# One call for each quarter of the hidden layer in place of one for two, in a convolution with top-1 mixture of experts

## The chip, the cores and the metric

The kernel runs on one core of a Trainium2 chip. The metric is the device time of one execution in microseconds (us). A core has five engines with a queue of instructions each: TensorE (PE, with its weight loads shown apart as PEld), VectorE (DVE), ScalarE (ACT), GpSimd (POOL) and SyncE (SP), which here only starts DMAs. [...]

## What is computed

`x` is 8 x 3584 rows of 192 numbers, 28,672 rows in all. First a causal convolution of 7 taps: each of 8 heads (24 columns each) has its own 7 weights, normalised by a softmax. Then a layer of 8 experts, of which each row uses one:

```python
logits = x @ w_gate                      # x is here the convolution's result
e_idx = np.argmax(logits, axis=1)
gate_w = softmax(logits)[row, e_idx]
eom = 1.0 / (1.0 + np.exp(-(x @ w_output_gate)))
for e in range(E):
    h = np.maximum(x[mask] @ w1[e], 0.0)   # 192 -> 1024
    ye = h @ w2[e]                         # 1024 -> 192
    out[mask] = gate_w[mask, None] * eom[mask, e, None] * ye
```

## The kernel before

**Front end.** The rows are cut into 16 units of 1,792 rows. For a unit, `front_a` does the convolution as 8 matmuls in float32 with banded weights (L290; each shows as two matmul records), copies the results out of PSUM as `cv`, transposes them with 24 small matmuls in 6 groups (L304), copies these as `tt`, multiplies by the gate weights (L313, a tile of 32 columns) and transposes back (L322). `front_b` finds each row's expert and weight on VectorE, counts with small matmuls (L361, L383 to L386), works out each row's place in its expert's stream (the rank chain, VectorE, L389 to L409), and then sorts the rows by permutation matmuls: `prep` makes the scaled rows `xrow` (L423) and the permutation `pm` (L428) on VectorE, L444 multiplies them, the result is copied out as `xs` (L278 on ScalarE or L280 on VectorE, in turn), and GpSimd scatters it to `xcg_sorted` in HBM (L462). Both are Python generators: each `yield` is a step that the main loop can place between other work.

**Slots.** A slot is 512 consecutive rows of one expert's stream, read back transposed as two overlapping pieces: `xa` holds columns 0 to 127, `xb` columns 64 to 191. Each unit from the third on has 4 slots, the last unit 8 and then 3 of 256 rows whose expert is chosen at run time (`pick`, L534 to L565, on VectorE). A last loop takes up what is left. `first` is the product 192 -> 1024. The 1024 hidden columns are four quarters of 2 x 128. Each of these two halves needs a matmul over 128 rows (`xa` or `xb`, L613) and one over the other 64 (L620): `xb[64:128]` or `xa[0:64]`[...]. A quarter takes one PSUM buffer `pp`[...]; the pool has two. A relu moves it to SBUF as `ht`: quarter 3 on VectorE (L631), the others on ScalarE (L633). `second(q)` is the product 1024 -> 192 for 128 of the rows: 8 matmuls of 192 columns (L655), and after each odd `q` a copy `y` (L661), which GpSimd scatters to the output (L482).

**Order of the work.** It is written out by hand; PE runs what it is given in that order. In the main loop a unit has 16 positions, `pos = 4 * k + q` for slot `k` and quarter `q`. At each position stand, in this order: `first` (before: at even `q` only, for two quarters), one step of `front_a` of the unit after next (positions 0 to 7 an L290, 8 to 10 an L304 group, 11 the L313), `second(q)` of the slot before, and then one step of the next unit's sort (positions 0 to 7), a second step of `front_a` (8 to 11: L304, at 11 L322) or a step of the following `front_b` (12 to 15: experts, counts, rank chain, first two `prep`). The small PSUM tiles of the front end, `pf`, have two buffers.

```python
for q in range(4):
    pos = 4 * k + q
    if q % 2 == 0:
        s.first(q // 2)
    drain(fa, 1)
    if prev is not None:
        prev.second(q)
```

Of the kernel before, what the change touches and what calls it, by code (L numbers as in the profile page):

```python
# [11 lines left out]
FP16 = mybir.dt.float16  # L12
FP32 = mybir.dt.float32
U32 = mybir.dt.uint32
AF = mybir.ActivationFunctionType
# [6 lines left out]
def kernel(  # L22
# [10 lines left out]
    nc = tc.nc  # L33
# [4 lines left out]
    F = moe_w1.shape[2]  # L38
# [10 lines left out]
    TT = 512  # L49
# [25 lines left out]
    ph = ctx.enter_context(tc.tile_pool(name="ph", bufs=2))  # L75
    pp16 = ctx.enter_context(tc.tile_pool(name="pp16", bufs=4))
    py = ctx.enter_context(tc.tile_pool(name="py", bufs=3))
    ps_h = ctx.enter_context(tc.tile_pool(name="ps_h", bufs=2, space=bass.MemoryType.PSUM))
# [60 lines left out]
    for h in (0, H // 2):  # L139
        for k in range(KW):  # L140
            m = idpu[:, k:k + BT]
            nc.vector.copy_predicated(
                out=band[:, h:h + H // 2, :],
# [60 lines left out]
    def load_w(e):  # L204
        o = e * WE
        w = moe_w1[e]
        nc.gpsimd.dma_start(
            wres[:, o:o + F].rearrange("p (l c) -> p l c", l=2),
            bass.AP(tensor=w.tensor, offset=w.offset,
                    ap=[[F, 128], [64 * F + F // 2, 2], [1, F // 2]]))  # L210
        nc.gpsimd.dma_start(wres[0:64, o + F:o + WA], w[0:64, F // 2:F])
        nc.gpsimd.dma_start(wres[64:128, o + F:o + WA], w[128:D, 0:F // 2])
        nc.gpsimd.dma_start(
            wres[:, o + WA:o + WE].rearrange("p (c d) -> p c d", d=D),
            moe_w2[e].rearrange("(c p) d -> p c d", p=128))
# [22 lines left out]
        out=o9, in_=bass.AP(tensor=eqe.tensor, offset=eqe.offset,  # L238
                            ap=[[eqe.ap[0][0], GE], [0, NG], [1, E + 1]]),
# [4 lines left out]
    for l in range(2):  # L244
        nc.vector.tensor_scalar(
            out=lsum[:, l * GE:(l + 1) * GE].rearrange("p (i e) -> p i e", e=E),
# [4 lines left out]
        out=lsum[:, c0 + NSEG:c0 + 2 * NSEG].rearrange("p (i e) -> p i e", e=E + 1),  # L251
# [216 lines left out]
    def emit_in(n=1):  # L468
        while n and pend:
            if last[0] == "in":  # L470
                nc.gpsimd.nop()
            pend.popleft()()
            last[0] = "in"
            n -= 1
# [3 lines left out]
    def emit_out():  # L478

        while pout:  # L480
            y, oi, j = pout.popleft()
            i = nc.gpsimd.indirect_dma_start(  # L482
                out=out, out_offset=bass.IndirectOffsetOnAxis(ap=oi[:, j:j + 1], axis=0),
                in_=y[:, j, :], in_offset=None, bounds_check=N - 1, oob_is_err=False)
            nodep(i, "out", ("out",))
            last[0] = "out"
# [81 lines left out]
    def slot_load(base, u, n=TT):  # L568
        skip = [f"sc{v}" for v in range(u + 1, NU)]
        xa = pxt.tile([128, TT], FP16, tag="xa", name="xa")[:, 0:n]  # L570
        xb = pxt.tile([128, TT], FP16, tag="xb", name="xb")[:, 0:n]
        xi = pxt.tile([128, 4, 2], FP16, tag="xi", name="xi")[:, 0:n // 128]
        i = nc.sync.dma_start_transpose(xa, xcg[bass.ds(base, n), 0:128])
        nodep(i, "load", skip)
        i = nc.sync.dma_start_transpose(xb, xcg[bass.ds(base, n), 64:192])
        nodep(i, "load", skip)
        i = nc.sync.dma_start(
            xi, xcg[bass.ds(base, n), IDC:IDC + 2].rearrange("(j p) w -> p j w", p=128))
        nodep(i, "load", skip)
        return xa, xb, xi  # L580
# [3 lines left out]
    def w_dyn(sel):  # L584

        if not wds:
            t = px.tile([128, NB, D], FP32, tag="xt", name="wd")
            t = t.rearrange("p c d -> p (c d)").bitcast(FP16)
            wds.extend(t[:, i * WE:(i + 1) * WE] for i in range(2 * NB * D // WE))
        wd = wds.pop(0)  # L590
        nc.sync.dma_start(wd, wres[:, bass.ds(reg(sel[0:1, 0:1], [ET.SP], (E - 1) * WE), WE)])
        return wd


    class Slot:
# [4 lines left out]
            self.nq = self.n // 128  # L600
            self.ht = []

        def first(self, q2):

            n, w = self.n, self.w
            pps = [ps_h.tile([128, 2, 512], FP32, tag="ph", name="pp")[:, :, 0:n]
                   for _ in range(2)]

            def rows128(r):
                o = (2 * q2 + r) * 128  # L610
                for l, x in enumerate((self.xa, self.xb)):
                    o2 = l * (F // 2) + o
                    nc.tensor.matmul(pps[r][:, l, :], w[:, o2:o2 + 128], x,  # L613
                                     start=(r == 0), stop=(r == 1))

            def rows64(r):

                c = F + (2 * q2 + r) * 128
                for l, (x, p0) in enumerate(((self.xb, 64), (self.xa, 0))):
                    nc.tensor.matmul(pps[r][:, l, :], w[p0:p0 + 64, c:c + 128], x[p0:p0 + 64],  # L620
                                     start=(r == 1), stop=(r == 0))

            rows128(0)
            rows64(0)
            rows64(1)
            rows128(1)
            for r in range(2):
                q = 2 * q2 + r
                ht = ph.tile([128, 2, TT], FP16, tag=f"ht{q}", name=f"ht{q}")[:, :, 0:n]
                if q == 3:  # L630
                    nc.vector.tensor_relu(out=ht, in_=pps[r])  # L631
                else:
                    nc.scalar.activation(out=ht, in_=pps[r], func=AF.Relu)  # L633
                self.ht.append(ht)

        def second(self, q):
            if q >= self.nq:
# [27 lines left out]
    def reg(ap, engines, hi):  # L665
        return nc.values_load(ap, engines=engines, min_val=0, max_val=hi,
                              skip_runtime_bounds_check_because="computed row of the stream")


    def drain(g, n=None):  # L670
        k = 0
        while n is None or k < n:
            try:
                next(g)
            except StopIteration:
                return False
            k += 1
        return True
# [9 lines left out]
    for u in range(U0 + 1):  # L688
# [5 lines left out]
        if u == 0:  # L694
# [3 lines left out]
            for e in range(E):  # L698
                i = nc.sync.dma_start(
                    out=xcg[e * CAP:e * CAP + TT, :].rearrange("(p g) w -> p (g w)", g=GR), in_=zrow)  # L700
# [4 lines left out]
    def loads(u):  # L705
        todo = []
        for e, bap, inv in plans.pop(u):
            base = reg(bap, [ET.SP], E * CAP - TT)
            todo.append((wres[:, e * WE:(e + 1) * WE], inv, slot_load(base, u)))
        if u == NU - 1:  # L710
            for sel, bap, inv in [pick(TP // 2) for _ in range(ND)]:
                base = reg(bap[0:1, 0:1], [ET.SP], E * CAP - TT)
                todo.append((w_dyn(sel), inv, slot_load(base, u, TT // 2)))
        return todo
# [11 lines left out]
    for u in range(U0, NU):  # L726
        fs, fa, fbn = fbn, iter(()), iter(())
        if u + 2 < NU:
            fa, fbn = front_a(u + 2), front_b(u + 2)
        nxt = None  # L730
        for k, (w, inv, xabi) in enumerate(todo):
            if 0 < 4 * (u - U0) + k <= EH:
                load_w(EH - 1 + 4 * (u - U0) + k)
            s = Slot(xabi, w, inv)
            for q in range(4):
                pos = 4 * k + q
                if q % 2 == 0:
                    s.first(q // 2)
                drain(fa, 1)
                if prev is not None:  # L740
                    prev.second(q)
                    emit_out()
                if pos < 8:
                    drain(fs, 1)
                elif pos < 12:
                    drain(fa, 1)
                else:
                    drain(fbn, 1)
                emit_in(len(pend))
                if pos == 7 and u + 1 < NU:  # L750
                    nxt = loads(u + 1)
            prev = s
        todo = nxt
# [20 lines left out]
    with tc.For_i(0, rn, 1):  # L774
        sel, bou, iu1 = pick(TP)
        base = reg(bou[0:1, 0:1], [ET.SP], E * CAP - TT)
        wds.clear()
        s = Slot(slot_load(base, NU), w_dyn(sel), iu1)
        for q2 in range(2):
            s.first(q2)  # L780
        for q in range(4):
            s.second(q)
            emit_out()
# [30 lines left out]
```

## Time and profile before

| | |
|---|---|
| median of 3 runs | 646.91 us (646.39 to 647.25) |
| the profiled execution | 647.25 us |
| its span on the core | 645.5 us |
| matmuls of `first`, 128 rows (L613, 512 columns) | 480, in 240 + 240 |
| matmuls of `first`, 64 rows (L620, 512 columns) | 480 |
| relus (L633 ScalarE, L631 VectorE) | 189 of 1001 ns, 63 of 1185 ns |
| matmuls of `second` (L655) | 1,968 |
| TensorE clock granted | 0.981 of full speed |

The page gives busy time by engine, the span in slices, the DMA queues, the chain of work that ended last, and groups of instructions by line. The end of a matmul's record is modelled and matmuls overlap, so how long TensorE is held is read between the starts of two matmuls that follow each other. "Idle before" is time in which an engine waited, and the name after the arrow is what released it.

### The profile page before, as it was taken

The page shows a single profiled execution, that of the slowest core. Times are in us where ns is not written, and L with a number is a line of the kernel's source. Part 1 is how long each engine was busy: PE and PEld are TensorE (multiplying, and loading weights), DVE is VectorE, ACT ScalarE, POOL GpSimd, SP SyncE. Part 2 cuts the span into 40 slices and gives each one's busy share as a digit, 9 for nine tenths or more (in the row PEclk, how much of TensorE's full clock was granted, in tenths as well). Part 3 has the DMA queues.
Part 4 walks back from the last instruction along what each step waited for, and adds up shares of the span by engine and source line. Part 5 has one row for each costly group of instructions (what it writes and reads, how often), then busy time and mean ns, then how long its engine had stood idle before and what let it go on. Part 6 is the DMA issues. An engine that isn't in the chain of part 4 may idle for free.

```text
span 645.5 us, 13578 instructions
## 1 busy us (share of the span) xinstructions
PE 586.5 (91%) x4544; PEld 360.3 (56%) x4544; DVE 406.3 (63%) x1362; ACT 355.4 (55%) x586; POOL 401.5 (62%) x419
## 2 busy tenths in 40 slices
PE   3998739999999999999999999999999999979993
PEld 1554415656665566656566566655566565546662
DVE  7567536584957658494775849577594956943332
ACT  1676525554665555556555555555555565656661
POOL 1362726876775756667476655756566674777773
PEclk9999859999999999999999999999999999999997
DMA  6979439994654647264553637355372525246631
GB/s 160 191 186 258 132 76 201 143 211 137 138 169 117 176 106 171 85 153 131 117 155 101 185 87 165 105 114 165 92 188 88 107 82 113 73 108 136 188 115 37
DMA packets 162569, 88.14 MB, mean 137 GB/s; under 512 B 116765, under 2 KB 153792, under 8 KB 162496
## 3 DMA queue, kind: packets, MB, share of 16 engines
q1 hardware_dynamic: 131872, 43.92, 30.3%
q0 software_dynamic: 29728, 43.30, 25.8%
q8 instruction: 36, 0.59, 0.4%
q14 instruction: 37, 0.30, 0.2%
q10 hardware_dynamic: 896, 0.03, 0.1%
HBM read 35.92 MB, written 43.06 MB: 122 GB/s over the span
## 4 chain that ended last, share of the span: by engine, by line
PE 66%; DVE 19%; ACT 6%; DMA 4%; issue 3%; SPq 0%; POOL 0%; DVEq 0%; ACTq 0%; POOLq 0%
PE pyt L655 18%; PE pp L613 13%; PE pf L290 11%; PE pp L620 8%; PE pf L444 5%; DVE ht L631 5%; PE pf L313 5%; PE pf L304 5%; ACT ht L633 4%; DVE xrow L423 2%; DVE pm L428 2%; DVE cv L280 2%; PE pf L322 2%; DMA out_dram<-y,oi 1%; DMA xt<-in_x_dram 1%
## 5 line engine op out<-in xcount | busy, mean ns | idle before, releaser
L482 POOL DMA_INDIRECT out_dram<-y,oi x246 | 245.6, 998 | 127.6 <-ACT y L661 63.4
L633 ACT ACTIVATE ht<-pp 128x1024 f16<-128x1024 f32 (+1 forms) x189 | 183.1, 1001 | 69.8 <-PE pp L620 67.0
L655 PEld LDWEIGHTS <-ht 128*128 128x128 f16 x1968 | 166.6, 98 | 58.2 <-issue 29.5
L655 PE MATMUL pyt<-wres,ht 128*128 128x192 f16 x1920 | 192.7, 246 | 1.5 <-DVE ht L631 1.5
L462 POOL DMA_INDIRECT xcg_sorted<-xs,du x128 | 131.5, 1027 | 92.2 <-DVE tk L502 22.1
L290 PE MATMUL pf<-xt,band 118*112 118x384 f32 x256 | 109.4, 523 | 19.1 <-DMA xt<-in_x_dram 10.8
L631 DVE TENSOR_SCALAR ht<-pp 128x1024 f16<-128x1024 f32 (+1 forms) x63 | 74.7, 1185 | 71.8 <-PE pp L613 71.8
L661 ACT COPY y<-pyt 128x384 f32<-128x384 f32 x123 | 59.0, 479 | 85.6 <-PE pyt L655 84.1
L613 PE MATMUL pp<-xa,wres 128*128 128x512 f16 x240 | 92.9, 387 | 9.1 <-DMA xa<-xcg_sorted 9.1
L613 PE MATMUL pp<-xb,wres 128*128 128x512 f16 x240 | 91.3, 380 | 1.2 <-DMA xb<-xcg_sorted 1.2
L620 PE MATMUL pp<-xb,wres 64*128 64x512 f16 x240 | 73.0, 383 | 1.6 <-ACT ht L633 1.2
L620 PE MATMUL pp<-xa,wres 64*128 64x512 f16 x240 | 73.0, 383 | 0.0
L444 PE MATMUL pf<-xrow,pm 112*128 112x194 f16 x512 | 65.1, 249 | 5.8 <-DVE pm L428 4.1
L613 PEld LDWEIGHTS <-wres 128*128 128x128 f16 x480 | 34.8, 97 | 60.7 <-issue 59.7
L290 PEld LDWEIGHTS pf<-xt,band 118*112 118x112 f32 x256 | 42.5, 185 | 41.6 <-DVE cv L280 11.5
L278 ACT COPY cv<-pf 112x384 f32<-112x384 f32 x80 | 38.1, 478 | 46.5 <-PE pf L290 38.6
L428 DVE TENSOR_SCALAR pm<-pos,pos 112x256 f16<-112x256 f16 x256 | 62.1, 307 | 0.0
L423 DVE TENSOR_TENSOR xrow<-cv,gs 112x384 f16<-112x384 f32 x121 | 61.9, 551 | 0.0
L444 PEld LDWEIGHTS <-pm 112*128 112x128 f16 x512 | 44.7, 98 | 15.3 <-DVE pm L428 7.7
L304 PE MATMUL pf<-identf,cv 112*128 112x112 f32 x384 | 50.7, 260 | 2.3 <-ACT tt L278 2.1
L278 ACT CAST xs<-pf 128x388 f16<-128x388 f32 x76 | 37.1, 492 | 27.5 <-PE pf L444 27.5
L304 PEld LDWEIGHTS pf<-identf,cv 112*128 112x128 f32 x384 | 40.9, 141 | 10.0 <-ACT tt L278 3.4
(139 smaller groups left out, 447.2 us busy)
## 6 DMA issues: line engine op xcount, KB each, us to landing
xt<-in_x_dram SPq DMA_DIRECT2D x8, 1344.0 KB
xt<-in_x_dram SPq DMA_DIRECT2D x8, 1260.0 KB
out_dram<-y,oi POOLq DMA_INDIRECT x246
wres<-in_moe_w_dram POOLq DMA_DIRECT2D x8, 384.0 KB
wd<-wres SPq DMA_DIRECT2D x3, 768.0 KB
wres<-in_moe_w_dram POOLq DMA_DIRECT2D x8, 256.0 KB
xcg_sorted<-xs,du POOLq DMA_INDIRECT x128
xcg_sorted<-zrow SPq DMA_DIRECT2D x8, 256.0 KB
```

Of the source, the lines that this page charges most:

```text
L278: nc.scalar.copy(out=o, in_=i)
L290: nc.tensor.matmul(pc[0:BT, 0:NB * GH], band[0:KI, h, :], xt[0:KI, :, h * GH:(h + 1) * GH], start=True, stop=True)
L304: nc.tensor.matmul(pt[:, j * BT:(j + 1) * BT], cvf[0:BT, m * 2 * D + i * 128:m * 2 * D + (i + 1) * 128], identf[0:BT, 0:BT], is_transpose= ...
L428: nc.vector.tensor_scalar(out=pms[i][P, l, :], in0=pos16[P], scalar1=pos[P, l * NG + i:l * NG + i + 1], scalar2=None, op0=ALU.is_equal)
L444: nc.tensor.matmul(ps[:, r * XW:(r + 1) * XW], pm[P, l, r * 128:(r + 1) * 128], xr[P, l * NG + i, :], start=(r == 0 and l == 0), stop=(r = ...
L462: i = nc.gpsimd.indirect_dma_start(out=xcg2, out_offset=bass.IndirectOffsetOnAxis(ap=du[:, i:i + 1], axis=0), in_=xs.rearrange("p r w -> p ...
L482: i = nc.gpsimd.indirect_dma_start(out=out, out_offset=bass.IndirectOffsetOnAxis(ap=oi[:, j:j + 1], axis=0), in_=y[:, j, :], in_offset=Non ...
L613: nc.tensor.matmul(pps[r][:, l, :], w[:, o2:o2 + 128], x, start=(r == 0), stop=(r == 1))
L620: nc.tensor.matmul(pps[r][:, l, :], w[p0:p0 + 64, c:c + 128], x[p0:p0 + 64], start=(r == 1), stop=(r == 0))
L631: nc.vector.tensor_relu(out=ht, in_=pps[r])
L633: nc.scalar.activation(out=ht, in_=pps[r], func=AF.Relu)
L655: nc.tensor.matmul(self.pp[:, o:o + D], self.ht[fc // 2][:, fc % 2, q * 128:(q + 1) * 128], self.w[:, w:w + D], start=(fc == 0 and q % 2 = ...
```

## The change

`first` takes one quarter `q` and is called at every position. Its matmuls run in the order 128 rows, 128 rows, 64 rows, 64 rows, and its relu follows at once. Before, a call took two quarters, in the order 128, 128, then four of 64 rows, then 128, 128, and the two relus followed. The loop at the end changes in the same way. Nothing else changes.

```diff
-        def first(self, q2):
-
+        def first(self, q):
             n, w = self.n, self.w
-            pps = [ps_h.tile([128, 2, 512], FP32, tag="ph", name="pp")[:, :, 0:n]
-                   for _ in range(2)]
...
-            rows128(0)
-            rows64(0)
-            rows64(1)
-            rows128(1)
-            for r in range(2):
-                q = 2 * q2 + r
...
+            o, o2, c = q * 128, F // 2 + q * 128, F + q * 128
+            pp = ps_h.tile([128, 2, 512], FP32, tag="ph", name="pp")[:, :, 0:n]
+            nc.tensor.matmul(pp[:, 0, :], w[:, o:o + 128], self.xa, start=True, stop=False)
+            nc.tensor.matmul(pp[:, 1, :], w[:, o2:o2 + 128], self.xb, start=True, stop=False)
+
+            nc.tensor.matmul(pp[:, 0, :], w[64:128, c:c + 128], self.xb[64:128],
+                             start=False, stop=True)
+            nc.tensor.matmul(pp[:, 1, :], w[0:64, c:c + 128], self.xa[0:64],
+                             start=False, stop=True)
+            ht = ph.tile([128, 2, TT], FP16, tag=f"ht{q}", name=f"ht{q}")[:, :, 0:n]
+            if q == 3:
+                nc.vector.tensor_relu(out=ht, in_=pp)
+            else:
+                nc.scalar.activation(out=ht, in_=pp, func=AF.Relu)
+            self.ht.append(ht)
@@
             for q in range(4):
                 pos = 4 * k + q
-                if q % 2 == 0:
-                    s.first(q // 2)
+                s.first(q)
                 drain(fa, 1)
@@
-        for q2 in range(2):
-            s.first(q2)
+        for q in range(4):
+            s.first(q)
         for q in range(4):
             s.second(q)
             emit_out()
```

More of the change, by code (lines that the diff above doesn't have):

```diff
@@ L601, in __init__ @@
             self.ht = []
-        def first(self, q2):
+        def first(self, q):
             n, w = self.n, self.w
-            pps = [ps_h.tile([128, 2, 512], FP32, tag="ph", name="pp")[:, :, 0:n]
-                   for _ in range(2)]
[L609 to L621, printed above, removed]
-            rows128(0)
-            rows64(0)
-            rows64(1)
-            rows128(1)
-            for r in range(2):
-                q = 2 * q2 + r
[L629 to L634, printed above, removed]
+            o, o2, c = q * 128, F // 2 + q * 128, F + q * 128
[12 more added lines that the diff above has]
+            self.ht.append(ht)
         def second(self, q):
```

## The prediction

> **What bounds the kernel now.** I read the page first: span, busy shares, chain.
>
> ```profile
> span 645.5 us, 13578 instructions
> PE 586.5 (91%) x4544; PEld 360.3 (56%) x4544; DVE 406.3 (63%) x1362; ACT 355.4 (55%) x586; POOL 401.5 (62%) x419
> PE 66%; DVE 19%; ACT 6%; DMA 4%; issue 3%; SPq 0%; POOL 0%; DVEq 0%; ACTq 0%; POOLq 0%
> ```
>
> TensorE carries two thirds of the chain. The busy table by stretch says where it is full:
>
> ```profile
> 300.00:400.00 100.00, 97.40 (x782) 60.23 (x780) 67.57 (x220) 56.33 (x90) 61.01 (x62) 1.00 0.49 125
> ```
>
> The columns are length, then PE, PE's loads, DVE, ACT and POOL. From 92 us to 621 us PE sets the pace, so each 0.1 us added to its order is paid. [...] The timeline of PE over one call of `first(q2)`:
>
> ```profile
> 300.79 0.38 PE L613 MATMUL pp<-xa,wres 128*128 128x512 f16 x1
> 301.01 0.38 PE L613 MATMUL pp<-xb,wres 128*128 128x512 f16 x1
> 301.32 0.39 PE L620 MATMUL pp<-xb,wres 64*128 64x512 f16 x1
> 301.32 0.39 PE L620 MATMUL pp<-xa,wres 64*128 64x512 f16 x1
> 301.54 0.38 PE L620 MATMUL pp<-xb,wres 64*128 64x512 f16 x1
> 301.55 0.38 PE L620 MATMUL pp<-xa,wres 64*128 64x512 f16 x1
> 301.85 0.39 PE L613 MATMUL pp<-xa,wres 128*128 128x512 f16 x1
> 302.08 0.38 PE L613 MATMUL pp<-xb,wres 128*128 128x512 f16 x1
> 302.30 0.55 PE L304 MATMUL pf<-identf,cv 112*128 112x112 f32 x4
> ```
>
> A 128-row matmul takes 0.22 us. Two 64-row ones start together and share one 0.22. Where the row count changes the step is 0.31: 0.09 more, on entering 64 rows (301.01 to 301.32) and on leaving (301.54 to 301.85). Over the trace the median steps are 310 and 308 ns (120 of each). Every other change of tile shape pays the same: L386 (64 rows) to L655 158 ns for 66 of work, L313 (32 columns) to L655 472 for about 376, L304 to L313 188 against 95.
>
> PE also waits, inside pairs of positions. Position 2k+1 has no first product, so its L290 follows L444 at once and finds its PSUM tile not yet copied out:
>
> ```profile
> 287.82 0.50 PE L444 MATMUL pf<-xrow,pm 112*128 112x194 f16 x4
> 289.06 0.90 PE L290 MATMUL pf<-xt,band 118*112 118x384 f32 x2 [0.73 <-DVE cv L280]
> ```
>
> [...] the L613 load starts at 300.70, ahead of its matmul; the loads of the two changes start with theirs, at 301.31 and 301.85; the 64-row matmuls start together at 301.32. [...] Here an f32 load of L290 takes 177 ns, an f16 one 98. [...]
>
> **The change, part by part.** The matmuls, relus and bytes are the same; no DMA is issued or moved. [...] Sums are against the profiled execution, 647.25 us (span 645.5 and 1.75 around it); the median of the runs is 646.91, 0.34 lower.
>
> (a) *Tile changes.* Before, a pair takes 1.505 us from its first start to the next work (median steps; 1.51 above). After, a quarter takes 0.22 + 0.31 + 0.00 + 0.31 = 0.84 to the start of the next work, two take 1.68: +0.175. There are 60 slots of 512 rows, 120 pairs: +21.0. The three half slots pay 0.16 for each of 6 pairs: +1.0. Where `first(3)` now stands directly before L313, the change to 32 columns was paid anyhow: -0.09 in each of 12 units, -1.1. Sum +20.9.
>
> (b) *Weights loaded in the open.* What now follows the 64-row matmuls is no longer always an f16 load. Where L290 started after a wait, with its load not ahead of it, its second matmul came 410 ns later instead of 326 (30 times): +0.085. L304 in that case 151 for 100 (6 times): +0.05. L655 after a known change of shape 93 for 82: +0.01. Each unit with a front has 8 exits to L290 and 3 to L304: 96 x 0.085 = 8.2, 36 x 0.05 = 1.8, 48 exits to L655 0.5. One L290 in each unit is hidden by wait (d), -1.0; the 30 and 6 of today go with their waits, -2.9. Sum +6.6. No run shows an f32 load after a 64-row tile. Bounds: 0 added [...] (then only the -2.9 stays), 9.5 [...]; I take the upper[...].
>
> (c) *Waits that go.* With a `first(q)` of 0.84 us between L444 and the next L290, and between L304 and L304 or L313, the copy has that time. By start-to-start steps over 92 to 545 us, L444 to L290 exceeds its 82 ns by 13.4 in all (longest 0.90), L304 to L304 its 95 by 3.4, L304 to L313 its 188 by 2.9. None is longer than 0.90, so I take 19.5 of the 19.7 as gone. ScalarE, with one relu (0.97) ahead of a copy in place of two, helps. Bounds: 15 if copies also come later, 19.7.
>
> (d) *Waits that come.* The relu of quarter 3 is VectorE's and moves one position later. At position 15 it now stands behind the rank chain of position 14 (L389 to L409), ahead of the first `xrow` and `pm` of the next unit's sort:
>
> ```profile
> 278.22 1.16 DVE L631 TENSOR_SCALAR ht<-pp 128x1024 f16<-128x1024 f32 x1
> ...
> 278.76 0.23 PE L386 MATMUL pf<-lsum,np 64*128 64x152 f16 x1
> ...
> 279.30 0.28 DVE L389 TENSOR_TENSOR dm<-pf,msk 112x128 f32<-112x128 f32 x1
> ...
> 281.89 0.99 DVE L428 TENSOR_SCALAR pm<-pos,pos 112x256 f16<-112x256 f16 x4
> 282.40 0.50 PE L444 MATMUL pf<-xrow,pm 112*128 112x194 f16 x4
> ```
>
> From L386's start: today the first `pm` is ready after 3.6 us and L444 starts after 3.64, no slack. After: rank chain 0.26 to 1.9, relu to 3.07, `xrow` (1.02) and two `pm` (0.49) to 4.42. PE reaches L444 after 0.16 + 0.84 + 0.66 + 0.84 + 0.74 + 0.66 = 3.9. Wait 0.5 to 0.55, 12 times: +6.6. Behind L444 stands all of PE's order. The same relu stands ahead of the `cv` copy in position 3; by the same walk it makes L290 of position 4 late by 0 to 0.5 in the six units whose `cv` copies are VectorE's: +1.5. Bounds of (d): 0 (another free PSUM tile and slack found) to 12.
>
> (e) *After 545 us*. Three `pick`s (14 VectorE instructions each, 561.4 to 569.6) hold the relu; PE's 3.3 us of waits there start with `loads` at position 7 and stay. Two waits for xa and xb at 575 (0.66 and 0.65) become shorter, -1.0; the last slots find quarter 3's relu closer to its use, about +0.3 each for three. I take 0. The loop at the end runs no round in this trace.
>
> Evacuation keeps up: a full slot after takes at least 6.0 us, ScalarE needs 3 x 0.97 + 2 x 0.48 = 3.9. A `pp` buffer is wanted again two calls later (3.0 us at the least), its relu ends 2.0 to 2.2 after the call's start.
>
> Sum: 20.9 + 6.6 - 19.5 + 8.1 + 0 = +16.1: 663.4 in the profiled run's terms, 663.0 against the median.
>
> **Rivals.** *R1[...].* (b) turns to -2.9, and PE, earlier, waits a little more in (d): 20.9 - 2.9 - 19.5 + 9 = +7.5, about 654.5 (651 to 657). [...] Against: an f32 load is 80 ns longer, and the open ones above show it.
> *R2, faster: even spacing wins.* The fused stage loses about 25 us to waits within units (2.1 in each of 12). If all of them go, no load is exposed and VectorE's shorter queue removes (d): 22 - 1.1 - 25.6 - 1.3 = -6, 641. It decides where the waits removed exceed the 20.9 of tile changes. Against it: the waits that a spacing of 0.84 us can touch sum to 19.7, below 20.9 before any exposed load.
> *R3, VectorE becomes the bound.* It is busy without a gap from 280.5 to 289 in the units that copy `cv` on it. If its late relu also stops `second(0)` of the next slot at fc 6, some 0.7 for half of the slots, +10 to +15 more: 675.
> *R4, no change*: (b) and (d) both near 0 in a sum of +1 or less.
>
> **How the numbers follow.** Chances: forecast 0.60 (its own range 657.5 to 669), R1 0.21, R2 0.06, R3 0.09, R4 0.04. The range 651 to 670 holds the forecast and R1, about 8 in 10. A measurement here can tell 0.2%, 1.3 us, from no change: faster 0.06, same 0.04, slower 0.90.
>
> **What would show it.** (a) After the change 252 entries and 252 exits with steps near 0.31, no 64-row pair followed by another. (b) The first L290 step after an exit near 0.41, not 0.33. (c) No [.. <-DVE cv] wait at odd positions. (d) A PE wait `<-DVE pm` at L444 at the start of each unit, near 0.5. A unit today takes 37.8 us (288.08 to 363.61 for two); I expect 38.9. Wrong if exits cost nothing where the shape changes back, or if a unit stays at 37.8.

## The result, and the profile after

The changed kernel takes 664.03 us (661.77 to 666.40, four runs) against 646.65 us for the kernel before: 1.027 times as long, with a 95% interval of 1.023 to 1.031. The forecast was 663.0. The profiled execution took 664.28 us, its span is 662.5, 17.0 more than before. Where a kernel's runs fall into a faster and a slower group, ratios in this document compare the faster ones.

The page after, the same three lines as before (span, busy shares, shares of the chain):

```profile
span 662.5 us, 13521 instructions
PE 614.9 (93%) x4544; PEld 363.5 (55%) x4544; DVE 409.4 (62%) x1362; ACT 356.0 (54%) x586; POOL 397.6 (60%) x419
PE 77%; DVE 13%; DMA 4%; issue 2%; ACT 1%; POOL 1%; SPq 0%; ACTq 0%; DVEq 0%; POOLq 0%
```

VectorE, ScalarE and GpSimd are as busy as they were, within 4 us. TensorE is busy 28 us longer with the same 4,544 matmuls, and its share of the chain rises from 66% to 77%. The timeline of PE over one quarter shows why (in the changed kernel L607 to L612 are the matmuls of `first`, L616 and L618 its relus on VectorE and ScalarE, and L640 is `second`, L655 before):

```profile
242.72 0.39 PE L607 MATMUL pp<-xa,wres 128*128 128x512 f16 x1
242.95 0.38 PE L608 MATMUL pp<-xb,wres 128*128 128x512 f16 x1
243.26 0.39 PE L610 MATMUL pp<-xb,wres 64*128 64x512 f16 x1
243.26 0.39 PE L612 MATMUL pp<-xa,wres 64*128 64x512 f16 x1
243.58 0.83 PE L640 MATMUL pyt<-wres,ht 128*128 128x192 f16 x8
```

242.72 to 243.58 is 0.86 us for one quarter (0.85 by the median steps), where a pair took 1.51. Both of its last two steps, 0.31 and 0.32, hold a change of tile shape, and there are 252 quarters.

Cut at the last L386 of a unit, the 17.0 us lie as follows. To the fifth unit's mark (127.76 us before, 126.13 after) 1.6 us are won. The eleven units to the last mark take 427.1 in place of 416.1, +11.0: two units together 77.65 in place of 75.53. From there to the last matmul it is 98.1 for 90.4, +7.7. What follows the last matmul is 11.3 in both. The cut itself shifts 0.85 us: quarter 3 of the slot stands ahead of this L386 before and behind it in the changed kernel. So the start wins 0.8 rather than 1.6, and the end loses 6.8 rather than 7.7.

### The profile page after: what moved, and what is told of

The parts are those of the page before. It is cut to its first block, busy times and chain, and to the rows that moved or that the text cites. A ratio compares the mean times of both kernels' runs of the same rounds, so it can differ in the third digit from the quotient of the medians.

```text
span 662.5 us, 13521 instructions
## 1 busy us (share of the span) xinstructions
PE 614.9 (93%) x4544; PEld 363.5 (55%) x4544; DVE 409.4 (62%) x1362; ACT 356.0 (54%) x586; POOL 397.6 (60%) x419
## 4 chain that ended last, share of the span: by engine, by line
PE 77%; DVE 13%; DMA 4%; issue 2%; ACT 1%; POOL 1%; SPq 0%; ACTq 0%; DVEq 0%; POOLq 0%
PE pyt L640 21%; PE pf L290 13%; PE pp L610 10%; PE pp L607 7%; PE pp L608 7%; PE pf L304 6%; PE pf L444 6%; PE pf L313 4%; DVE xrow L423 3%; DMA out_dram<-y,oi 2%; DVE ht L616 2%; DVE pm L428 2%; PE pf L322 1%; DVE xs L280 1%; DMA wg<-n_moe_w_output_gate_dram 0%
## 5 line engine op out<-in xcount | busy, mean ns | idle before, releaser
L482 POOL DMA_INDIRECT out_dram<-y,oi x246 | 244.8, 995 | 149.8 <-ACT y L646 87.6
L618 ACT ACTIVATE ht<-pp 128x1024 f16<-128x1024 f32 (+1 forms) x189 | 189.5, 1003 | 104.9 <-PE pp L612 103.8
L640 PE MATMUL pyt<-wres,ht 128*128 128x192 f16 x1920 | 200.2, 247 | 4.0 <-DVE ht L616 4.0
L640 PEld LDWEIGHTS <-ht 128*128 128x128 f16 x1968 | 160.7, 98 | 71.2 <-issue 51.5
L462 POOL DMA_INDIRECT xcg_sorted<-xs,du x128 | 128.4, 1003 | 90.4 <-DVE tk L502 22.7
L290 PE MATMUL pf<-xt,band 118*112 118x384 f32 x256 | 115.0, 545 | 10.6 <-DMA wg<-n_moe_w_output_gate_dram 10.6
L616 DVE TENSOR_SCALAR ht<-pp 128x1024 f16<-128x1024 f32 (+1 forms) x63 | 75.5, 1198 | 67.0 <-PE pp L612 66.0
L607 PE MATMUL pp<-xa,wres 128*128 128x512 f16 x240 | 92.3, 384 | 8.8 <-DMA xa<-xcg_sorted 8.8
L612 PE MATMUL pp<-xa,wres 64*128 64x512 f16 x240 | 93.6, 390 | 0.0
L610 PE MATMUL pp<-xb,wres 64*128 64x512 f16 x240 | 93.6, 390 | 0.0
L610 PEld LDWEIGHTS <-wres 64*128 64x128 f16 x240 | 22.2, 92 | 103.8 <-issue 103.8
L444 PE MATMUL pf<-xrow,pm 112*128 112x194 f16 x512 | 66.3, 249 | 7.6 <-DVE pm L428 7.2
L290 PEld LDWEIGHTS pf<-xt,band 118*112 118x112 f32 x256 | 38.2, 183 | 40.5 <-issue 21.4
L280 DVE COPY tt<-pf 128x448 f32<-128x448 f32 x36 | 22.5, 625 | 53.4 <-PE pf L304 53.4
L444 PEld LDWEIGHTS <-pm 112*128 112x128 f16 x512 | 44.3, 98 | 20.1 <-DVE pm L428 13.0
L304 PE MATMUL pf<-identf,cv 112*128 112x112 f32 x384 | 53.3, 265 | 0.2 <-ACT cv L278 0.2
```

The lines of the kernel that those rows point to most:

```text
L290: nc.tensor.matmul(pc[0:BT, 0:NB * GH], band[0:KI, h, :], xt[0:KI, :, h * GH:(h + 1) * GH], start=True, stop=True)
L304: nc.tensor.matmul(pt[:, j * BT:(j + 1) * BT], cvf[0:BT, m * 2 * D + i * 128:m * 2 * D + (i + 1) * 128], identf[0:BT, 0:BT], is_transpose= ...
L444: nc.tensor.matmul(ps[:, r * XW:(r + 1) * XW], pm[P, l, r * 128:(r + 1) * 128], xr[P, l * NG + i, :], start=(r == 0 and l == 0), stop=(r = ...
L462: i = nc.gpsimd.indirect_dma_start(out=xcg2, out_offset=bass.IndirectOffsetOnAxis(ap=du[:, i:i + 1], axis=0), in_=xs.rearrange("p r w -> p ...
L482: i = nc.gpsimd.indirect_dma_start(out=out, out_offset=bass.IndirectOffsetOnAxis(ap=oi[:, j:j + 1], axis=0), in_=y[:, j, :], in_offset=Non ...
L607: nc.tensor.matmul(pp[:, 0, :], w[:, o:o + 128], self.xa, start=True, stop=False)
```

## The experiments

Two theories stood at the start. T is the prediction's: changes of tile shape and weight loads in the open cost more than the waits that go. V says that the order of VectorE's and ScalarE's work is what costs. H, a part of R1, says that after an exit the load of L290's float32 weights adds nothing to what the change of shape takes. A load is called open where it starts with its matmul: in the kernel before, L290's load starts 214 ns ahead behind a 128-row matmul, and its first step is 327 ns (47 places); behind a wait it starts 2 ns ahead, and the step is 413 (31 places).

Where the kernel before ran beside the first four kernels it took 759 us, and 766 beside quarter_act_slot3 and pair_late_front_act, on two other chips, with stalls of up to some 5 us that the trace gives no local cause for. The traces from there also show 44 to 102 us with TensorE granted half its clock, from 100 us on to the last matmul, where the kernel before at 647 us shows none; their mean clock is 0.913 to 0.954, its 0.981. From those traces I take steps and waits, and times only beside the kernel before; four of the kernels were measured again where it takes 647.

**Spacing alone.** Both orders without any change of tile shape in `first`: one 128-row matmul in place of the two 64-row ones, in the kernel before and in the changed one. Both leave out the product's real 64-row part. The edit of the changed kernel (that of the kernel before does the same in its own form):

```diff
-            nc.tensor.matmul(pp[:, 0, :], w[64:128, c:c + 128], self.xb[64:128],
-                             start=False, stop=True)
-            nc.tensor.matmul(pp[:, 1, :], w[0:64, c:c + 128], self.xa[0:64],
-                             start=False, stop=True)
+            nc.tensor.matmul(pp[:, 1, :], w[:, c:c + 128], self.xb, start=False, stop=True)
...
```

> The kernel before with each pair of 64-row matmuls replaced by one 128-row matmul of the same 512 columns (so the product's 64-row part is wrong), no change of tile shape left in first. Theory T (the time is tile changes plus loads in the open, less waits): 126 x 0.187 us of entries and exits go, 23.5; with PE faster some waits grow by 0 to 6: 623 to 629 us. Theory V (what costs is the order of VectorE's and ScalarE's queues, not the shapes): about 645.

> The changed kernel with the same replacement (the 64-row part is wrong in the same way): one call for each quarter, no change of tile shape in first. Against pair_128 only the spacing of the calls differs. T: faster than pair_128 by 8 to 16 us, 610 to 620, since the waits inside pairs (19.7 us before) go and the wait of L444 (6.6 us) stays. V: slower than pair_128 or equal.

Beside a 759 us kernel before, pair_128 took 756.65 us and quarter_128 737.14. Measured again:

> As pair_128 (the kernel before, each pair of 64-row matmuls replaced by one of 128 rows, so that part of the product is wrong), measured again where the kernel before takes its usual 647 us. T (tile changes plus loads in the open, less waits): 623 to 629 us. V (order of the queues, not the shapes): about 645.

> As quarter_128 (the changed kernel with the same replacement), measured again. Against pair_128_2 only the spacing of the calls differs. T: faster than pair_128_2 by 8 to 16 us, 610 to 620. V: not faster.

pair_128_2: 632.75 us (0.977 of before, 0.974 to 0.979). quarter_128_2: 624.05 (0.963, 0.959 to 0.966). Both are some 4 us above T's ranges. Waits are one reason: with TensorE faster, the first L444 of a unit waits 0.24 in nine units of the first and 0.90 in nine of the second, and from 92 us on L444's waits come to 5.4 us (1.9 before) and 11.6 (6.6 in the changed kernel). In the first that is within the 0 to 6 that T allowed. The other reason is the clock: ahead of the last matmul TensorE was granted half its clock for 23.9 and 27.3 us in these two traces, for 17.1 in that of the kernel before (mean clock over the span 0.973, 0.971 and 0.981). By my estimate, from each step's excess over the usual one of its kind, these stretches cost 5.4, 9.0 and 3.4 us. The difference decides: one call for each quarter is 8.7 us *faster* when no shape changes, and the clock was against it. V, that the order of the queues is the main cost, falls. And the shapes are worth 646.85 - 632.75 = 14.1 us in the kernel before, 664.03 - 624.05 = 40.0 in the changed one (with the loads that they leave open and the waits that these take up): 25.9 more. 25.9 less 8.7 is 17.2, as it must be, since these four times hold the whole change; what they show is that its two parts have opposite signs.

**Shapes alone.** The calls stay where they were; only the order within the pair changes (the start and stop flags, not shown, follow it).

```diff
             rows128(0)
             rows64(0)
-            rows64(1)
             rows128(1)
+            rows64(1)
```

> The kernel before, calls of two quarters at even positions as they were, but in the order 128, 128, 64, 64, 128, 128, 64, 64: two entries and exits for a pair in place of one, spacing untouched. T: +21 for the changes, +4.1 for 48 exits to L290, +1.2 for 24 to L304, some of it taken by waits: 669 to 675 us. V: 647 to 650. Theory H [...]: 666 to 669, and steps of 326 ns at L290 after an exit.

> As pair_two_changes (the kernel before with 128, 128, 64, 64, 128, 128, 64, 64 in a pair), measured again. T: 669 to 675 us. V: 647 to 650. H [...]: 666 to 669; its traced steps of 413 ns between the two matmuls of L290 speak against H already.

pair_two_changes was 762.59 us beside 759.34; measured again it is 662.53 (1.025 of before, 1.023 to 1.026), below T's range and H's. The timeline of PE, the second half of a pair and what follows:

```profile
290.77 0.39 PE L613 MATMUL pp<-xa,wres 128*128 128x512 f16 x1
290.99 0.38 PE L613 MATMUL pp<-xb,wres 128*128 128x512 f16 x1
291.31 0.39 PE L620 MATMUL pp<-xb,wres 64*128 64x512 f16 x1
291.31 0.39 PE L620 MATMUL pp<-xa,wres 64*128 64x512 f16 x1
291.62 0.90 PE L290 MATMUL pf<-xt,band 118*112 118x384 f32 x2
292.36 0.82 PE L655 MATMUL pyt<-wres,ht 128*128 128x192 f16 x8
```

The changes cost what T says, 0.32 and 0.31, and L290 after an exit holds TensorE 0.74 us (291.62 to 292.36), not 0.65, so H falls. But the waits took up more: L444 to L290 exceeds its 82 ns by 3.5 us in this trace, where it was 13.4 before. Of the 13.4, 10.3 are waits for a copy `cv` by VectorE and 2.7 for one by ScalarE; 1.8 and 0.4 of them are left here. In this trace what the slower TensorE added to its own work came off its waits for copies that other engines make. T had the costs right and the cover too small.

**Loads in the open.** The changed kernel with the order of its four matmuls turned round, so that every exit from 64 rows is to an f16 load.

```diff
-            nc.tensor.matmul(pp[:, 0, :], w[:, o:o + 128], self.xa, start=True, stop=False)
-            nc.tensor.matmul(pp[:, 1, :], w[:, o2:o2 + 128], self.xb, start=True, stop=False)
             nc.tensor.matmul(pp[:, 0, :], w[64:128, c:c + 128], self.xb[64:128],
-                             start=False, stop=True)
+                             start=True, stop=False)
             nc.tensor.matmul(pp[:, 1, :], w[0:64, c:c + 128], self.xa[0:64],
-                             start=False, stop=True)
+                             start=True, stop=False)
+            nc.tensor.matmul(pp[:, 0, :], w[:, o:o + 128], self.xa, start=False, stop=True)
+            nc.tensor.matmul(pp[:, 1, :], w[:, o2:o2 + 128], self.xb, start=False, stop=True)
```

> The changed kernel with the 64-row matmuls ahead of the 128-row ones in each quarter: as many changes of shape, but every exit is to an f16 load of 128 rows. T: 96 x 0.087 for L290, 36 x 0.05 for L304, 1 to 2 for the rest go: 9 to 12 us less, 652 to 655. H: no gain, 663 to 665.

> As quarter_64first (the changed kernel with the 64-row matmuls first in each quarter, every exit to an f16 load), measured again. T: 652 to 655 us. H: 663 to 665.

quarter_64first was 745.83 us beside 759.34. Measured again it is 656.12, 1.014 of before (1.013 to 1.016), 7.9 below the changed kernel: 1 us short of T, H falls again. What TensorE's load queue waited for ahead of L290 (us, times), with "issue" for no releaser in the profile: in the kernel before,

```profile
  issue: 2.5, 8
```

in the changed one,

```profile
  issue: 21.4, 90
```

and in quarter_64first_2:

```profile
  issue: 1.8, 6
```

The changed kernel shows it 90 times, and 96 of its L290 follow an exit. Part of the gain went into L444's wait for `pm`, 0.69 in place of 0.40 in nine units.

**The wait for pm.** The prediction's step (d) put it down to the place of VectorE's relu behind the rank chain. The first edit puts that relu ahead of the chain again.

```diff
-            if q == 3:
+            if q == 2:
                 nc.vector.tensor_relu(out=ht, in_=pp)
```

> The changed kernel with VectorE's relu on quarter 2 in place of quarter 3, so that at position 14 it stands ahead of the rank chain again. T (the time is tile changes plus loads in the open, less waits): the waits of L444 on pm (12 of 0.40 and 6 of 0.23) go: 6 us less, 657 to 659. V (the order of VectorE's queue is the main cost): 10 us or more less, below 654.

662.64 us, 1.4 below the changed kernel, within its spread; L444's wait is still 0.41 in ten units, and the second one (0.23 at position 1, for the copy `xs`) is 0.19. The same unit in both traces, first the changed kernel:

```profile
244.49 1.22 DVE L616 TENSOR_SCALAR ht<-pp 128x1024 f16<-128x1024 f32 x1
245.63 1.02 DVE L423 TENSOR_TENSOR xrow<-cv,gs 112x384 f16<-112x384 f32 x2
246.49 1.01 POOL L482 DMA_INDIRECT out_dram<-y,oi  x1 [0.30 <-issue]
246.56 0.99 DVE L428 TENSOR_SCALAR pm<-pos,pos 112x256 f16<-112x256 f16 x4
246.90 0.62 PE L444 MATMUL pf<-xrow,pm 112*128 112x194 f16 x4 [0.23 <-DVE pm L428]
```

and quarter_relu2, where L616 ran ahead of the chain, at 243.05:

```profile
245.78 1.02 DVE L423 TENSOR_TENSOR xrow<-cv,gs 112x384 f16<-112x384 f32 x2
245.80 1.39 POOL L482 DMA_INDIRECT out_dram<-y,oi  x1 [1.45 <-ACT y L646]
246.71 1.03 DVE L428 TENSOR_SCALAR pm<-pos,pos 112x256 f16<-112x256 f16 x4
247.29 0.51 PE L444 MATMUL pf<-xrow,pm 112*128 112x194 f16 x4 [0.25 <-DVE pm L428]
```

Counted from L361's start, `pm` starts at 5.93 us in the changed kernel and at 5.70 in quarter_relu2, as in the kernel before (5.71). So the place of the relu is worth 0.23. But in those ten units the first of the `pm` instructions takes 0.52 us in place of 0.28, while GpSimd's L482 beside it takes 1.39 in place of 1.01, and L444 starts no earlier: 6.28 in place of 6.27. In the one unit where it takes 0.32, the wait is 0.21. Why the two are slow together is not shown. TensorE's side counts too. It came to L444 at 6.23 before, without a wait, and without a wait comes at 5.87 now (6.27 less 0.40), because one quarter and not a pair lies ahead of L444 at position 0. An estimate from these figures: with `pm` as early as before, L444 could start at 6.04 (it does in pair_128_2), so of the wait of 0.40 some 0.17 come from TensorE and 0.23 from the place of the relu. The next edit takes the relu out of the stretch.

```diff
+            s.act = k == 3 and u + 2 < NU
...
-            if q == 3:
+            if q == 3 and not self.act:
                 nc.vector.tensor_relu(out=ht, in_=pp)
```

> The changed kernel with all four relus of a unit's fourth slot on ScalarE in place of three, in the 12 units with a front. That takes 1.16 us out of VectorE's work between L361 and the first L444, which a move of the relu to quarter 2 left there. If that work, with less of TensorE's to cover it, is what L444 waits for, the 12 waits of 0.40 and with them 0.23 in six units go: 657 to 659 us. If the wait has another cause it stays: 662 to 664.

Its time, 746.63 us beside 765.84, can't be set against the changed kernel's, of which there is no trace from that place. But steps and waits can be compared: in all 12 units L444's wait is 3 ns or less; in ten it comes 5.87 us after L361, and there `pm` starts at 4.80 to 5.19 in place of 5.93. quarter_64first, in a trace with the same stalls and its relu on VectorE, has waits of 0.69 to 1.12 there. What L444 waited for (us, times), in the changed kernel,

```profile
PEld L444 <- DVE pm L428: 13.0, 22, 2.4
PE pf L444 <- DVE pm L428: 7.2, 15, 1.8
```

and in quarter_act_slot3:

```profile
PEld L444 <- DVE pm L428: 5.0, 6, 2.4
PE pf L444 <- DVE pm L428: 3.3, 3, 1.8
```

What is left lies ahead of 70 us, in the fill before the main loop. Without the relu `pm` starts up to 1.13 us earlier than in the changed kernel, with the relu in another place 0.23.

**A better order.** If waits inside pairs cost 20 us and changes of shape must not be doubled, the pair should stay and something else come between. At odd positions `second(q)` can.

```diff
+                late = q % 2 == 1 and pos < 11
+                if not late:
+                    drain(fa, 1)
-                drain(fa, 1)
                 if prev is not None:
                     prev.second(q)
                     emit_out()
+                if late:
+                    drain(fa, 1)
```

> The kernel before, with the step of front_a behind second(q) in place of ahead of it at the odd positions up to 9. The 0.66 us of second now lie between L444 and the next L290, and between two groups of L304. T: of the waits inside pairs 12 of 13.4 us go, 3 of L304, and 2.5 us of loads in the open with them: 630 to 634 us. V: the wait moves to L444 or to the next copy: 643 to 647.

642.02 us (638.09 to 645.32), 0.993 of before (0.990 to 0.996): 4.5 us below the kernel before, and not T's 12 to 16. Its seven runs differ in the clock that they were granted; the three that had 0.980 or more, as most runs of the kernel before did, took 638.1 to 639.3. The L304 waits went (3.7 us to 0.3). L290's moved on, 4.6 us to L290 behind `second` and 6.7 to the L444 behind it (8.5 where it was 1.8). The timeline of DVE and PE at position 1:

```profile
241.42 1.02 DVE L423 TENSOR_TENSOR xrow<-cv,gs 112x384 f16<-112x384 f32 x2
241.62 0.82 PE L290 MATMUL pf<-xt,band 118*112 118x384 f32 x2
...
242.36 0.48 DVE L428 TENSOR_SCALAR pm<-pos,pos 112x256 f16<-112x256 f16 x2
...
242.75 0.55 DVE L280 CAST xs<-pf 128x388 f16<-128x388 f32 x1
...
243.36 0.49 PE L444 MATMUL pf<-xrow,pm 112*128 112x194 f16 x4 [0.92 <-DVE xs L280]
```

L444 waits for the copy `xs`, and that stands behind `xrow` and `pm` on VectorE. In this trace the new place mostly changes who waits; that VectorE's load in the first positions of a unit is the cause is argued from it and not tested on its own. A last edit gave ScalarE the relus of the first and fourth slot, and of unit 14 (with `and not self.act` in `first`, as above):

```diff
+            s.act = (k in (0, 3) and u + 2 < NU) or u == NU - 2
```

> pair_late_front with all relus of the first and fourth slot of a unit, and of unit 14, on ScalarE. If VectorE is what L444 and L290 still wait for at positions 1 and 3 (0.75 and up to 1.08 us in six units, 0.31 more), 6 to 10 us go there, and 2 to 3 where unit 14's picks hold VectorE: 630 to 635 us. If those waits have another cause: 638 to 643.

753.81 us beside 765.84, 0.987 (0.979 to 0.995). Whether it beats pair_late_front where the kernel before takes 647 us stays open.

## Why the prediction was right, point by point

The forecast was 663.0, the result 664.03, and the mechanism was right in the main: shapes and open loads cost more than the waits that go. How the terms did, by start-to-start steps over the whole trace:

(a) *Tile changes, +20.9.* Confirmed as a cost, and about 2 too small: +22.7. 240 entries take 310 ns, but exits 316 to 318 where I had taken the 308 of an exit after two 64-row pairs. Where L313 follows it is 316 to 317 in all, so its own change came free, as forecast. In the slots after the last front I took 0.35 a slot, they take 0.43 (6.08 us for 5.65), because each of the four exits is 10 ns longer and each first step of `second` after it 93 ns for 82, a load in the open that I had counted in the front's units alone. "Every other change of tile shape pays the same" goes too far: after the very short matmuls of the counts the step grows by less, 103 ns for 52 from L361 to L613 and 123 for 60 from L384 to L385.

(b) *Loads in the open, +6.6.* Right in kind, and about 8 in size. The first step of L290 is 413 ns in nearly all of the 96 places, its load starting 2 ns ahead of it, L304's 151 after an exit. That an open load costs as much behind a change of shape as behind a wait was my estimate from L655 (93 ns for 82); for L290 the 413 of both shows it. None of the L290 was hidden by a wait, for which I had taken off 1.0. 64-rows-first takes the open loads away and gains 7.9. "No run shows an f32 load after a 64-row tile" was a misreading: in the fill of the kernel before, at 29.3, 45.7 and 60.8 us, an L290 follows the 64-row L386 without a wait, and its first step is 413 or 414 ns. So the trace of before already spoke against R1.

(c) *Waits that go, -19.5.* They all went; after an exit no L290 waits over 0.25 us. But of 19.4 us of these waits (by my count) some 12 are gone in pair_two_changes_2 too, where the calls stand as before and TensorE is slower. Spacing and slowness came together here, and (c) credits all to spacing.

(d) *Waits that come, +8.1.* The wait for `pm` came as walked through: 0.40 us at the first matmul of L444 and 0.11 more at its second, which needs the second `pm`, so 0.51 in each of eleven units for the 0.5 to 0.55 forecast, and 6.8 us in all with the last unit (1.07, of which 0.58 stood there before). VectorE kept the order that the prediction assumed: `xrow` starts at 245.63, behind the relu that starts at 244.49 and takes 1.22. TensorE's 290 matmul records stand in the same order in eleven units of each trace, so what waits at L444 holds up all behind it. The relu behind the chain is part of the cause, as the runs above show, and TensorE's earlier arrival the other. Two smaller things differ: five waits of 0.23 at position 1 for the copy `xs` were not forecast, and the wait for `cv` at position 4 (1.5) didn't come.

(e) *After 545 us, 0.* From the last L386 to the last matmul it is +7.7. 0.85 of it is the shift of the cut; 12 slots at 0.43 and three half slots at about 0.3, which belong to (a) and (b), are 6.1. The rest, +0.7, is a balance: TensorE's waits there fell from 7.2 us to 6.2, and from 583.3 to 586.7 us, after a wait of 3.0 us for the relu behind VectorE's `pick`s, it was granted half its clock, which by its steps cost 1.5 us. The kernel before has no such stretch there. My 0 left out the clock.

(a) and (b) together came out some 3 us larger than forecast, (d) some 0.8 smaller, and what I had put at 0 (the start, the end and smaller waits) some 1.6 lower, so that the sum came within 1 us is in part luck.

A unit takes 38.8 us; I had expected 38.9. R1 falls with the 413 ns, R2's mechanism is real but measures 8.7 us against shapes' 25.9, R3's further stop of `second(0)` is not in the trace but for the `pick`s.

## What to carry to other kernels

Put matmuls of the same tile shape together before you space work out: on this kernel a change of shape in `first` held TensorE for about 0.09 us, and what followed an exit paid for its weight load too (11 ns more for the float16 of `second`, 87 for the float32 of L290), so let a float16 matmul follow the odd shape (7.9 us in quarter_64first_2). Before you break a block of work up, list what runs on another engine under it: here half a block no longer covered what the whole did (TensorE came to L444 after 5.87 us in place of 6.23 and waited 0.40), and that engine's whole work over the stretch counted for more than the place of one instruction (1.13 us against 0.23). Waits for another engine were taken up by slower work (pair_two_changes_2) and handed on by a new order (pair_late_front); the wait for `pm` ended when that engine had less to do (quarter_act_slot3).

## What the runs showed that I had not expected

An exit from 64 rows after one 64-row pair takes 318 ns to an f16 load, after two pairs 308; the same next matmul, L613, takes 308 in the kernel before and 318 to 319 in pair_two_changes_2. After an exit the first step of L655 is 93 ns for 82, and of L290 413 for 326: an f16 weight load left in the open cost 11 ns here, a float32 one 87.

Where the kernel before took 759 to 766 us, kernels with one call for each quarter came out below it: quarter_128 0.967 of before (0.957 to 0.978), quarter_64first 0.976 (0.963 to 0.989) and quarter_act_slot3 0.983 (0.975 to 0.991), while pair_128, with less work, was no faster at 1.008 (1.001 to 1.014). Why engines stalled there was not settled, and there is no time of the changed kernel itself from there.
